# Attention and gated MLP in four chunks: one chunk's input transposed on TensorE instead of by DMA, chunk 0's products in halves, and a new order of the work

## The chip, the core and the metric

The kernel runs on one core of a Trainium2 chip. A core has engines that each work through their own queue of instructions in order: TensorE (PE; its weight loads are shown apart as PEld), VectorE (DVE), ScalarE (ACT), GpSimd (POOL) and SyncE (SP), which here only issues DMAs. They meet through semaphores. The metric is the device time of one execution in microseconds (us): 200.8 is the median of three runs of the kernel before (200.71 to 200.93).

## The reference

One layer on x of 2048 rows by 512 columns, all in bf16:

```python
h  = x + A(layernorm(x))          # attention
h2 = h + B(layernorm(h))          # gated MLP

# A: qkv = x @ wqkv, 32 heads of 16; each row looks at 8 rows: itself and
#    those 2, 4, ... 14 above it (masked where there is none)
logits = einsum("bhsd,bhswd->bhsw", q, k_gathered) * 16 ** -0.5
o = einsum("bhsw,bhswd->bhsd", softmax(logits), v_gathered)
A = o @ wo
# B: F = 1376
gate = x @ W_gate; up = x @ W_up
B = (relu(gate) * up) @ W_down
```

## The kernel before, in words

The 2048 rows are worked in four chunks of 512 (`tk` in the code, "chunk 0" to "chunk 3" here). In a chunk the steps are:

- **Layer norm of x** (`layernorm`, key `x...`): statistics (`bn_stats`, L431, and L434) and the normalised row (L466) on DVE, four tiles of 128 rows. Then the tile is transposed, so that columns stand on partitions. This goes either through TensorE (four 128x128 transposes a tile, L495, and a copy out of the PSUM bank by ScalarE, L511, or for two tiles of chunk 0 by DVE, L509) or by a DMA transpose that SP issues (L484). The table `DMAT` (L348) lists the pairs of tiles that go by DMA; it has chunk 3's x, and the second norm (`h`) of chunks 2 and 3 and half of chunk 1's.
- **Projections** (L536): twelve groups of four matmuls, q and k for four groups of columns in turn and then v, each into a PSUM bank that ScalarE copies out (L544). For the first four groups of chunk 0 (`n < 4`) each group is made in two column halves, rows 0 and 1 of tiles first (`qka`), rows 2 and 3 after (`qkc`), over all four blocks of the weight.
- **Scores**: DVE multiplies q with the four shifted k of one half of the window (L583, `pr`), for two groups of columns at once: 4096 elements a partition. TensorE sums over a head's columns (L589, `sc`, four matmuls of 32 columns at a time), ScalarE takes exp (L619), and for chunk 0 DVE masks (L622, `mk`).
- **Weights back to all columns**: TensorE broadcasts (L689, `bc`) and ScalarE copies (L695) for chunks 0 and 1; for chunks 2 and 3 SP's DMAs do it (L679, `bd`).
- **Weighted v**: DVE multiplies the eight weights with the eight shifted v (L710, `mu`, 4096 elements). The eight are then summed by a tree: its first level (eight to four) is for chunks 0 to 2 a DMA that accumulates, issued by POOL (L742, `ta`), the rest DVE adds (L713, L736), and for chunk 0 a scaling (L717, `om`).
- **Output projection** (L762, `wo`), for chunk 0 with x added by one more matmul (L765), the second layer norm (ScalarE squares, L420), up and gate matmuls (L800) with ScalarE's copies (L804, L807) and DVE's product (L820), the down matmuls (L837), the last addition (L848) and the store (L854).

Every step is recorded first as an `Op` with its engine, planned duration, what it depends on and which buffer of a pool it takes. `Plan.order()` then lays them out: each engine's queue goes by the priorities of the list `RANK`, one number for each recorded step, and the planner picks the next step and a buffer by planned times. The steps are issued in that order, so an instruction waits on its engine for all that stand ahead of it, and the planner's times (`xload`, `wload`, the DMA queue term `dq`) have no effect on the chip but through that order and through the choice of buffers. The one exception is `setup()`, which issues all loads ahead of everything; the weight of q and k comes in four blocks of 128 rows, two issued by SP and two by ScalarE (L294).

So TensorE has in its queue projections of later chunks between the steps of chunk 0's attention, and where they stand decides whether it waits.

Of the kernel before, what the change touches and what calls it, by code (L numbers as in the profile page):

```python
# [8 lines left out]
P = 128  # L9
# [4 lines left out]
ALU = mybir.AluOpType  # L14
# [4 lines left out]
    0, 1, 2, 3, 4, 5, 6, 7, 8, 9, 10, 11, 12, 13, 14, 15, 16, 18, 19, 21,  # L19
    24, 32, 27, 17, 20, 22, 25, 26, 30, 35, 36, 29, 34, 37, 39, 41, 43, 47, 23, 28,  # L20
    31, 33, 38, 45, 48, 42, 59, 65, 40, 51, 55, 46, 56, 60, 49, 52, 57, 73, 76, 61,
    79, 67, 72, 71, 74, 80, 106, 88, 95, 75, 96, 91, 104, 103, 93, 113, 119, 127, 70, 85,
    94, 98, 102, 172, 175, 185, 130, 134, 136, 149, 152, 105, 108, 110, 114, 111, 188, 197, 223, 226,
    231, 179, 190, 217, 221, 228, 171, 180, 208, 211, 219, 158, 169, 195, 207, 210, 245, 252, 236, 241,
    239, 244, 243, 249, 256, 260, 247, 253, 246, 250, 255, 261, 266, 269, 276, 281, 275, 279, 285, 278,
    283, 282, 286, 291, 310, 315, 326, 330, 293, 322, 314, 324, 348, 329, 361, 337, 345, 339, 342, 346,
    350, 365, 333, 358, 349, 354, 340, 352, 353, 356, 363, 323, 328, 316, 321, 302, 313, 308, 312, 332,
    364, 373, 366, 370, 306, 379, 369, 394, 405, 359, 393, 355, 380, 402, 404, 421, 442, 445, 395, 424,
    453, 574, 374, 413, 447, 450, 389, 409, 436, 473, 50, 53, 44, 62, 54, 64, 58, 63, 66, 69,
    77, 90, 78, 83, 92, 81, 87, 82, 86, 89, 118, 129, 157, 170, 124, 196, 164, 178, 97, 101,  # L30
    166, 182, 100, 116, 150, 159, 132, 186, 107, 176, 137, 156, 109, 126, 200, 213, 218, 237, 232, 240,
    251, 258, 262, 264, 274, 284, 287, 288, 296, 294, 292, 298, 300, 307, 305, 309, 303, 318, 327, 360,
    367, 311, 319, 341, 347, 336, 343, 372, 377, 325, 334, 368, 375, 382, 385, 384, 388, 381, 383, 386,
    398, 390, 392, 397, 400, 387, 396, 401, 403, 406, 407, 408, 411, 414, 417, 410, 418, 412, 419, 422,
    457, 467, 434, 484, 477, 480, 461, 481, 491, 472, 475, 429, 466, 449, 460, 441, 476, 478, 433, 435,
    454, 458, 446, 451, 439, 443, 462, 474, 503, 427, 431, 469, 486, 502, 505, 508, 493, 512, 465, 525,
    507, 518, 511, 521, 529, 497, 516, 504, 513, 520, 531, 552, 569, 572, 524, 541, 666, 707, 514, 533,
    537, 540, 536, 539, 580, 708, 112, 120, 99, 121, 68, 84, 115, 122, 125, 133, 144, 163, 147, 160,
    165, 142, 148, 135, 145, 161, 229, 234, 233, 242, 187, 202, 177, 199, 174, 183, 192, 194, 184, 189,
    206, 235, 212, 215, 181, 191, 193, 205, 214, 238, 289, 265, 297, 317, 248, 257, 290, 301, 331, 335,  # L40
    338, 357, 344, 362, 371, 415, 425, 456, 459, 423, 432, 464, 470, 430, 438, 468, 471, 391, 399, 448,
    455, 479, 483, 490, 495, 485, 492, 482, 488, 487, 489, 499, 501, 494, 496, 498, 506, 509, 515, 519,
    522, 526, 528, 527, 534, 517, 532, 596, 601, 562, 594, 565, 589, 558, 591, 604, 544, 553, 542, 551,
    555, 560, 548, 550, 570, 549, 557, 546, 556, 579, 583, 568, 573, 586, 599, 608, 609, 614, 571, 576,
    603, 611, 618, 617, 626, 613, 629, 588, 631, 606, 627, 632, 620, 624, 585, 616, 635, 639, 662, 668,
    672, 623, 641, 643, 677, 628, 636, 638, 675, 634, 637, 645, 647, 117, 141, 128, 139, 131, 140, 123,
    138, 143, 146, 155, 162, 153, 167, 168, 173, 151, 154, 204, 225, 254, 268, 273, 299, 259, 270, 209,
    227, 216, 220, 267, 280, 224, 230, 201, 222, 198, 203, 263, 272, 271, 277, 304, 295, 320, 376, 378,
    351, 416, 420, 426, 428, 437, 444, 440, 463, 452, 530, 535, 543, 561, 500, 510, 523, 566, 547, 554,
    564, 567, 538, 545, 559, 563, 593, 597, 575, 578, 577, 581, 582, 587, 600, 602, 590, 598, 584, 595,  # L50
    592, 605, 607, 610, 619, 622, 615, 625, 621, 633, 612, 630, 657, 689, 683, 687, 667, 673, 671, 680,
    692, 640, 656, 658, 660, 648, 654, 650, 661, 664, 676, 679, 644, 652, 678, 682, 655, 663, 684, 649,
    651, 653, 670, 642, 646, 665, 669, 674, 694, 696, 685, 693, 659, 690, 681, 686, 698, 691, 699, 688,
    697, 701, 710, 714, 717, 719, 705, 709, 711, 715, 695, 702, 704, 706, 700, 703, 712, 713, 716, 718,
    720, 721,
# [36 lines left out]
class Plan:  # L92
# [23 lines left out]
    def order(self):  # L116
# [6 lines left out]
        free = {}  # L123
# [7 lines left out]
        while left:  # L131
# [36 lines left out]
            op.start, op.done = t, t + op.dur + op.lat  # L168
            if op.dq:
                at = max(t + op.dur + op.dq[0], free.get("DQ", 0.0)) + op.dq[1]  # L170
                free["DQ"] = at
                op.done = at + op.lat
            free[op.eng] = t + op.dur
# [18 lines left out]
def kernel(  # L192
# [11 lines left out]
    nc = tc.nc  # L204
# [11 lines left out]
    PRE = ()  # L216
    NAB = 0
# [127 lines left out]
    DAL = 5.5  # L345
    TDD, TDL = 1.25, 1.5
    NWARM, NFILL = 44, 8
    DMAT = (('h',2,0),('h',2,2),('x',3,0),('x',3,2),('h',3,0),('h',3,2),('h',1,0))  # L348
# [11 lines left out]
    HG = ([[0, 1, 2, 3]],) * 4  # L360

# [12 lines left out]
    def load(t):  # L374
        return add(None, "LD", 0.0, None, lat=t)

    xload = [[load(t) for t in (3.5, 3.7, 4.1, 4.35)]] + [[load(t)] * BPC for t in (9.15, 13.2, 15.4)]
    wload = {n: load(t) for n, t in
             (("q", 7.78), ("k", 7.78), ("v", 10.6), ("o", 17.1), ("u", 20.5), ("g", 24.0), ("d", 28.5))}
# [139 lines left out]
    for tk in range(NCK):  # L519
# [10 lines left out]
        for n, (c, t) in enumerate(seq):  # L530
# [3 lines left out]
            def f_mm(lo=0, hi=CS, c=c, t=t, mm=mm, xnT=xnT):  # L534
                for dt in range(NT):
                    nc.tensor.matmul(mm.t[:, lo:hi], lhsT=wv_sb[:, dt, t:D:NT] if c == 2 else wqk_sb[:, dt, c * D + t:(c + 1) * D:NT],  # L536
                                     rhs=xnT.t[:, dt, lo:hi], start=(dt == 0), stop=(dt == NT - 1))
# [9 lines left out]
            if tk == 0 and n < 4:  # L547

                a = None
                for i, (lo, hi, evs) in enumerate(((0, 2 * P, xev[0:2]), (2 * P, CS, xev[2:]))):  # L550
                    a = add(("qk%s%d" % ("ac"[i], n), tk), "PE", 4 * MM * (hi - lo) / CS + 0.02,
                            lambda f=f_mm, lo=lo, hi=hi: f(lo, hi), evs + [wl, a, fills[-1]], pr - 5, take=[mm],
                            use=[xnT], lat=PEL if i == 1 else 0.0)
            else:
                a = add(("qkv%d" % n, tk), "PE", 4 * MM, f_mm, xev + [wl], pr, take=[mm], use=[xnT], lat=PEL)
# [13 lines left out]
        for hf in range(2):  # L569
            sc, ex = Buf(at_s), Buf(ex_s)  # L570
            scd, prd = [], []
            for t in range(0, NT, 2):
# [13 lines left out]
                def f_sc(t=t, sc=sc, pb=pb):  # L586
                    for u in range(2):
# [5 lines left out]
                a = add(("pr%d" % hf, tk), "DVE", D40, f_pr, [d[k] for k in (t, t + 1) for d in (qd, kd, kp)],  # L593
                        apr, take=[pb], use=[qT], lat=DL)
# [312 lines left out]
```

## Time and profile before

| | |
|---|---|
| median of three runs | 200.8 us |
| the profiled execution | 201.23 us, of which the span of its instructions is 199.5 |
| TensorE clock granted | 1.0 of full |
| TensorE from 20 to 180 us, in windows | idle in 1.2 us of 160 |
| VectorE from 20 to 80 us, in windows | idle in 0.6 us of 60 |
| VectorE from 140 to 199.5 us | busy 22.9 us of 59.5 |
| ScalarE | 115.0 us of the span |
| DMA: accumulates issued by POOL | 12 of 512 KB |
| DMA transposes issued by SP | 14, landing 2.5 us after their issue (median) |

A line of the page's group table has the source line, the engine, the operation, what is written and read, the shape and the count; then busy time in all, the mean of one in ns, and how long the engine stood idle just ahead of these instructions and what ended that. Matmuls overlap in the pipeline, so one that lasts 379 ns is followed by the next after 216. The chain of waits goes back from the last instruction to what released it, step by step. A timeline row has the start, the time from first start to last end, engine, line, and the count of instructions merged into it.

### The profile page before, as it was taken

The page shows a single profiled execution, that of the slowest core. Times are in us where ns is not written, and L with a number is a line of the kernel's source. Part 1 is how long each engine was busy: PE and PEld are TensorE (multiplying, and loading weights), DVE is VectorE, ACT ScalarE, POOL GpSimd, SP SyncE. Part 2 cuts the span into 40 slices and gives each one's busy share as a digit, 9 for nine tenths or more (in the row PEclk, how much of TensorE's full clock was granted, in tenths as well). Part 3 has the DMA queues.
Part 4 walks back from the last instruction along what each step waited for, and adds up shares of the span by engine and source line. Part 5 has one row for each costly group of instructions (what it writes and reads, how often), then busy time and mean ns, then how long its engine had stood idle before and what let it go on. Part 6 is the DMA issues. An engine that isn't in the chain of part 4 may idle for free.

```text
span 199.5 us, 2918 instructions
## 1 busy us (share of the span) xinstructions
PE 191.6 (96%) x1080; PEld 95.7 (48%) x1099; DVE 152.6 (77%) x239; ACT 115.0 (58%) x240; POOL 12.6 (6%) x28
## 2 busy tenths in 40 slices
PE   8599999999999999999999999999999999999994
PEld 8385445554445344444444444444444444444542
DVE  6669999999999999998899859999964423032332
ACT  3455899881999987663844557701439620456500
POOL 4000000330000004100113000000000000000000
PEclk9999999999999999999999999999999999999999
DMA  6959981897000008985269970140010130102022
GB/s 166 327 185 324 412 283 32 156 192 148 3 0 0 3 0 157 190 165 123 39 118 196 208 204 2 26 85 20 3 53 0 26 79 0 31 0 79 0 79 79
DMA packets 19981, 20.92 MB, mean 105 GB/s; under 512 B 8608, under 2 KB 16768, under 8 KB 19968
## 3 DMA queue, kind: packets, MB, share of 16 engines
q1 hardware_dynamic: 17520, 13.60, 23.0%
q0 software_dynamic: 1728, 6.29, 16.8%
q10 hardware_dynamic: 720, 0.85, 1.6%
q8 instruction: 8, 0.13, 0.3%
q14 instruction: 5, 0.04, 0.1%
HBM read 8.42 MB, written 2.10 MB: 53 GB/s over the span
## 4 chain that ended last, share of the span: by engine, by line
PE 91%; DMA 4%; ACT 2%; issue 1%; SPq 1%; DVE 0%
PE bank L800 37%; PE bank L536 21%; PE bank L837 19%; PE bank L762 7%; DMA wqk_sb<-in_A_wqkv_dram 4%; PE bank L589 3%; PE bank L495 2%; ACT big L695 1%; PE bank L639 1%; ACT quad L511 1%; PE bank L765 0%; SPq L292 0%; PE bank L689 0%; ACT quad L544 0%; SPq L294 0%
## 5 line engine op out<-in xcount | busy, mean ns | idle before, releaser
L800 PE MATMUL bank<-quad,wu_sb 128*128 128x512 bf16 (+1 forms) x170 | 42.7, 379 | 0.7 <-ACT quad L511 0.3
L800 PE MATMUL bank<-quad,wg_sb 128*128 128x512 bf16 (+1 forms) x173 | 41.6, 379 | 0.1
L837 PE MATMUL bank<-wd_sb,gT 128*128 128x512 bf16 (+3 forms) x184 | 39.4, 366 | 0.2
L807 ACT ACTIVATE gr<-bank 128x512 bf16<-128x512 f32 (+1 forms) x44 | 25.3, 601 | 23.3 <-PE bank L800 21.8
L804 ACT CAST up_sb<-bank 128x512 bf16<-128x512 f32 (+1 forms) x44 | 25.1, 588 | 23.2 <-PE bank L800 22.4
L710 DVE TENSOR_TENSOR big<-big,vT 128x4096 bf16<-128x4096 bf16 x16 | 36.1, 2290 | 0.8 <-DMA big<-ex 0.6
L583 DVE TENSOR_TENSOR big<-quad,kT 128x4096 bf16<-128x4096 bf16 x16 | 36.2, 2288 | 0.4 <-ACT quad L544 0.4
L536 PE MATMUL bank<-quad,wqk_sb 128*128 128x512 bf16 (+1 forms) x140 | 30.3, 356 | 2.1 <-DMA wqk_sb<-in_A_wqkv_dram 1.8
L820 DVE TENSOR_TENSOR gT<-gr,up_sb 128x1024 bf16<-128x1024 bf16 (+1 forms) x24 | 15.2, 646 | 20.5 <-ACT up_sb L804 10.4
L837 PEld LDWEIGHTS <-gT 128*128 128x128 bf16 (+1 forms) x187 | 18.2, 98 | 19.7
L800 PEld LDWEIGHTS <-wu_sb 128*128 128x128 bf16 (+1 forms) x176 | 17.5, 100 | 21.1 <-issue 1.3
L800 PEld LDWEIGHTS <-wg_sb 128*128 128x128 bf16 (+1 forms) x176 | 17.6, 100 | 20.5 <-issue 0.2
L536 PEld LDWEIGHTS <-wqk_sb 128*128 128x128 bf16 x144 | 15.5, 114 | 14.3 <-DMA wqk_sb<-in_A_wqkv_dram 2.3
L848 DVE TENSOR_TENSOR row<-x_sm,bank 128x512 bf16<-128x512 bf16 (+1 forms) x17 | 10.8, 653 | 10.6 <-PE bank L837 10.6
L713 DVE TENSOR_TENSOR big<-big 128x1024 bf16<-128x1024 bf16 (+2 forms) x24 | 17.2, 735 | 0.7 <-DMA big<-big 0.6
L742 POOL DMA_DIRECT2D big<-big x12 | 10.5, 872 | 86.8 <-DVE big L710 42.7
L536 PE MATMUL bank<-quad,wv_sb 128*128 128x512 bf16 x62 | 15.2, 380 | 0.1
L762 PE MATMUL bank<-wo_sb,quad 128*128 128x512 bf16 x63 | 15.2, 379 | 0.1
L466 DVE TENSOR_SCALAR row<-x_sm,mv,rs 128x512 bf16<-128x512 bf16 x32 | 11.6, 407 | 2.3 <-ACT rs L448 2.1
L431 DVE BATCH_NORM_STATS2 st<-x_sm 128x6 f32<-128x512 bf16 x16 | 10.5, 680 | 3.4 <-DMA x_sm<-in_A_x_dram 3.4
L420 ACT ACTIVATE row<-x_sm,mv 128x512 bf16<-128x512 bf16 x12 | 8.6, 723 | 5.0 <-DVE mv L412 5.0
L544 ACT CAST kT<-bank 128x512 bf16<-128x512 f32 x16 | 9.2, 592 | 3.4 <-PE bank L536 3.4
(68 smaller groups left out, 141.6 us busy)
## 6 DMA issues: line engine op xcount, KB each, us to landing
big<-big POOLq DMA_DIRECT2D x12, 512.0 KB, 5.5
big<-ex SPq DMA_DIRECT2D x16, 128.0 KB, 2.8
out_dram<-row SPq DMA_DIRECT2D x15, 128.0 KB, 1.8
x_sm<-in_A_x_dram SPq DMA_DIRECT2D x3, 512.0 KB, 6.4
wu_sb<-in_B_W_up_dram SPq DMA_DIRECT2D x1, 1376.0 KB, 9.7
wg_sb<-in_B_W_gate_dram SPq DMA_DIRECT2D x1, 1376.0 KB, 12.7
wd_sb<-in_B_W_down_dram SPq DMA_DIRECT2D x1, 1280.0 KB, 15.7
wqk_sb<-in_A_wqkv_dram ACTq DMA_DIRECT2D x2, 256.0 KB, 7.2
```

The lines of the kernel that those rows point to most:

```text
L466: V.tensor_scalar(out=xn.t[:], in0=x, scalar1=mv.t[:, j, 0:1], scalar2=rs.t[:, j:j + 1], op0=ALU.add if residual else ALU.subtract, op1=AL ...
L536: nc.tensor.matmul(mm.t[:, lo:hi], lhsT=wv_sb[:, dt, t:D:NT] if c == 2 else wqk_sb[:, dt, c * D + t:(c + 1) * D:NT], rhs=xnT.t[:, dt, lo:h ...
L583: V.tensor_tensor(out=pb.t[:].rearrange("p (t w) s -> p t w s", t=2), in0=q4, in1=k4, op=ALU.mult)
L710: V.tensor_tensor(out=mt.t[:], in0=ab.t[:], in1=v8, op=ALU.mult)
L713: V.tensor_tensor(out=mt.t[:, 0:n, :], in0=mt.t[:, 0:n, :], in1=mt.t[:, n:2 * n, :], op=ALU.add)
L762: nc.tensor.matmul(od.t[:], lhsT=OT.t[:, t, j * P:(j + 1) * P], rhs=wo_sb[:, t, :], start=(t == 0), stop=(t == NT - 1 and tk not in RPE))
L800: nc.tensor.matmul(mm.t[:fs, :], lhsT=w_sb[:, dt, ft * P: ft * P + fs], rhs=hnT.t[:, dt, :], start=(dt == 0), stop=(dt == NT - 1))
L804: nc.scalar.copy(out=ub.t[:fs, i, :], in_=um.t[:fs, :])
L807: nc.scalar.activation(out=gr.t[:fs, i, :], in_=gm.t[:fs, :], func=ACT.Relu)
L820: V.tensor_tensor(out=gt.t[:fs, 0:n, :], in0=gr.t[:fs, 0:n, :], in1=ub.t[:fs, 0:n, :], op=ALU.mult)
L837: nc.tensor.matmul(od.t[:, c0:c1], lhsT=gts[ft].t[:fs, ft % 2, j * P:(j + 1) * P], rhs=wd_sb[:fs, ft, c0:c1], start=(ft == 0), stop=(ft == ...
L848: V.tensor_tensor(out=ob.t[:, c0:c1], in0=x_sm[:, tk * BPC + j, c0:c1], in1=od.t[:, c0:c1], op=ALU.add)
```

## The change

Three things change in the recorded steps, and with them the order of everything:

1. Chunk 3's x leaves `DMAT`: its four tiles are transposed by sixteen TensorE transposes, with two ScalarE copies, and four DMA transposes on SP go.
2. Chunk 0's first four projection groups are made in three parts: both column halves over weight blocks 0 and 1 only (`qka`, `qkc`, two matmuls of 256 columns each, which wait for those two blocks alone), then the full width over blocks 2 and 3 (`qkd`).
3. Chunk 0's q*k products (`PRS`) and weight*v products (`MUH`) are made by two instructions of 2048 elements each in place of one of 4096. A q*k half needs one group of q and k; a weight*v half needs one half of the window.

The planner's load times and its model of the DMA queue are changed too, and `RANK` is a new list (737 numbers in place of 722). The further options `PRD`, `DAC2` and `HSP` come in with empty lists.

```diff
-    DMAT = (('h',2,0),('h',2,2),('x',3,0),('x',3,2),('h',3,0),('h',3,2),('h',1,0))
+    DMAT = (('h',2,0),('h',2,2),('h',3,0),('h',3,2),('h',1,0))
+    PRS, MUH = (0,), (0,)
...
-            def f_mm(lo=0, hi=CS, c=c, t=t, mm=mm, xnT=xnT):
-                for dt in range(NT):
+            def f_mm(lo=0, hi=CS, d0=0, d1=NT, c=c, t=t, mm=mm, xnT=xnT):
+                for dt in range(d0, d1):
                     nc.tensor.matmul(mm.t[:, lo:hi], lhsT=...,
-                                     rhs=xnT.t[:, dt, lo:hi], start=(dt == 0), stop=(dt == NT - 1))
+                                     rhs=xnT.t[:, dt, lo:hi], start=(dt == 0 and lo == 0), stop=(dt == NT - 1))
...
-                a = None
+                ab, done = [wload["ab"]], []
                 for i, (lo, hi, evs) in enumerate(((0, 2 * P, xev[0:2]), (2 * P, CS, xev[2:]))):
-                    a = add(("qk%s%d" % ("ac"[i], n), tk), "PE", 4 * MM * (hi - lo) / CS + 0.02,
-                            lambda f=f_mm, lo=lo, hi=hi: f(lo, hi), evs + [wl, a, fills[-1]], pr - 5, take=[mm],
-                            use=[xnT], lat=PEL if i == 1 else 0.0)
+                    done.append(add(("qk%s%d" % ("ac"[i], n), tk), "PE", 2 * MM * (hi - lo) / CS + 0.005,
+                                    lambda f=f_mm, lo=lo, hi=hi: f(lo, hi, 0, 2), evs + ab + done + [fills[-1]], pr - 5,
+                                    take=[mm], use=[xnT]))
+                a = add(("qkd%d" % n, tk), "PE", 2 * MM, lambda f=f_mm: f(0, CS, 2, NT), done + [wl], pr - 4.9, take=[mm],
+                        use=[xnT], lat=PEL)
...
+                if tk in PRS:
+                    def f_p1(u, t=t, hf=hf, pb=pb, qT=qT, s0=s0):
+                        kb = kT[:, t + u, PADL + s0 - 4 * hf * DIL: PADL + s0 - 4 * hf * DIL + CS]
+                        k4 = bass.AP(tensor=kb.tensor, offset=kb.offset,
+                                     ap=[list(kb.ap[0]), [-DIL, 4]] + [list(y) for y in kb.ap[1:]])
+                        V.tensor_tensor(out=pb.t[:, 4 * u:4 * u + 4, :],
+                                        in0=qT.t[:, t + u, :].unsqueeze(1).to_broadcast([P, 4, CS]), in1=k4, op=ALU.mult)
+                    for u in range(2):
+                        a = add(("pr%d%s" % (hf, "ac"[u]), tk), "DVE", D20, lambda u=u, f=f_p1: f(u),
+                                [d[t + u] for d in (qd, kd, kp)], apr, take=[pb], use=[qT], lat=DL)
...
+            if tk in MUH:
+                def f_m1(hf, t=t, ab=ab, mt=mt, s0=s0):
+                    vb = vT[:, t, PADL + s0 - 4 * hf * DIL: PADL + s0 - 4 * hf * DIL + CS]
+                    ...
+                    V.tensor_tensor(out=mt.t[:, 4 * hf:4 * hf + 4, :], in0=ab.t[:, 4 * hf:4 * hf + 4, :], in1=v4, op=ALU.mult)
+                ms = [add(("mu%d%s" % (t, "ac"[hf]), tk), "DVE", D20, lambda hf=hf, f=f_m1: f(hf),
+                          [x for x in abd if x.key[0][2] == str(hf)] + vds, tpr, take=[mt], use=[ab], lat=DL) for hf in range(2)]
```

What the order does with it, by engine. On TensorE, all four tiles of chunk 0 are transposed ahead of the first q/k group (before, two were behind the first two groups); chunk 3's transposes stand among chunk 2's projections; chunk 0's output projection comes after four of chunk 3's twelve projection groups in place of six; chunk 2's first scores and chunk 1's first broadcast, which followed each other, have the transposes of two tiles between them; and between chunk 0's second transposes and its first up matmul there now stand two broadcasts, one projection and one score group, where there were a broadcast and a score group. On VectorE, the copy L509 of tile 3 comes ahead of chunk 1's statistics, chunk 0's half products follow each other in another order, and chunk 2's statistics go behind chunk 0's first products. On SP, chunk 3's broadcasts go out ahead of all of chunk 0's stores. POOL's twelve accumulates stay, in another order within chunks 1 and 2.

## The prediction, made before the changed kernel had run

> **What bounds the kernel now.** I read the page's busy table first, then the chain that ended last, then windows and the timeline at the places where the chain leaves the matmuls, and last the DMA landings.
>
> ```profile
> span 199.5 us, 2918 instructions
> PE 191.6 (96%) x1080; PEld 95.7 (48%) x1099; DVE 152.6 (77%) x239; ACT 115.0 (58%) x240; POOL 12.6 (6%) x28
> PE 91%; DMA 4%; ACT 2%; issue 1%; SPq 1%; DVE 0%
> ```
>
> The chain is TensorE (PE) nearly from end to end. What PE doesn't do is wait for the first weights, in the chain in order of time (start, length, what) and in PE's timeline:
>
> ```profile
> 2.16 7.84 DMA wqk_sb<-in_A_wqkv_dram
> 10.05 0.85 PE bank L536 x6
> 10.89 0.45 PE bank L495 x8
> 64.90 0.47 ACT quad L511
> ```
>
> ```profile
> 8.66 0.41 PE L536 MATMUL bank<-quad,wqk_sb 128*128 128x256 bf16 x2 [0.85 <-DMA wqk_sb<-in_A_wqkv_dram]
> 10.05 0.85 PE L536 MATMUL bank<-quad,wqk_sb 128*128 128x256 bf16 x6 [0.98 <-DMA wqk_sb<-in_A_wqkv_dram]
> 53.23 1.03 PE L762 MATMUL bank<-wo_sb,quad 128*128 128x512 bf16 x4
> 66.88 1.02 PE L800 MATMUL bank<-quad,wu_sb 128*128 128x512 bf16 x3 [0.27 <-ACT quad L511]
> ```
>
> Two of four weight blocks are there at 8.66, and PE uses them for two matmuls only; the other two come at 10.05. Behind that PE is full, so the end is set by (a) how much PE work is left at 10.05, and (b) whether VectorE (DVE) feeds it in time. DVE has little room up to the first output projection (L762, 53.23), as the window from chunk 1's x to the end of chunk 0's attention shows:
>
> ```profile
> core 0: us, PE busy (x) PEld busy (x) DVE busy (x) ACT busy (x) POOL busy (x), PEclk, DMA share, GB/s
> 11.15:52.18 41.03, 40.76 (x261) 21.98 (x264) 40.13 (x62) 31.08 (x61) 3.76 (x5) 1.00 0.75 207
> ```
>
> ```profile
> 35.41 6.69 DVE L710 TENSOR_TENSOR big<-big,vT 128x4096 bf16<-128x4096 bf16 x3
> 51.43 0.75 DVE L717 TENSOR_TENSOR quad<-big,rec 128x512 bf16<-128x512 bf16 x2
> ```
>
> ```profile
> L710 DVE TENSOR_TENSOR big<-big,vT 128x4096 bf16<-128x4096 bf16 x16 | 36.1, 2290 | 0.8 <-DMA big<-ex 0.6 <-issue 0.2
> L713 DVE TENSOR_TENSOR big<-big 128x2048 bf16<-128x2048 bf16 x4 | 4.9, 1222 | 0.1
> ```
>
> The profiled execution took 201.23 us, its span 199.5; the median of the runs shown is 200.8. I sum differences against the profiled execution and carry them to the median.
>
> **PE work, part by part.** *Start.* In the new order the transposes of rows 2 and 3 stand before the first q/k matmul, and each of the four q/k banks first gets its products over weight blocks 0 and 1. PE then has, before 10.05, eight transposes (0.45, chain row) and ten 256-column matmuls (eight first halves, one bank's second pair; 0.109 each by start times at 10.3 to 10.6): 0.45 + 1.09 = 1.54 in place of today's two (0.22): 1.32 us of work is gone from behind 10.05. It fits: the two rows leave DVE at 7.97 and 8.35 (L466), so their transposes end at about 8.6; their two copies (0.59 and 0.41, on ScalarE and DVE) end by about 9.4, before the second pair wants them; 8.66 + 1.09 = 9.75. Sixteen of 32 half-width matmuls become eight full ones: 16 x 0.109 - 8 x 0.216 = 0.02 less.
>
> *Stalls of today that lose their cause.* By matmul start times PE loses 0.17 at 12.2 (VectorE's copy L509 stands behind a bn_stats that waits for x; now ahead of it) and 0.22 at 14.2 (a bank): 0.39. At 66.9 and 69.3 it loses 0.33 and 0.18 to the copy L511 of chunk 0's transposes: there the new order puts a score group, two broadcasts and a projection between the last transposes and the first up matmul (about 2.7 us against 1.5), more than the two copies need (2 x 1.02): 0.51.
>
> *Chunk 3's transposes.* 16 more on PE. The chain has eight in 0.45, so 0.056 each: +0.89. They need two more ScalarE copies (1.016 each); ScalarE is busy 7.38 of 12.18 between 40 and 52.18, so they hide; if that cover went they would cost at most 2.0. Four DMA transposes leave SP's queue (1.2 each); SP is otherwise idle there, so nothing directly. *Order.* Chunk 2's scores and chunk 1's broadcast no longer touch, so one more change between the packed form and full matmuls: 0.10 by start times (0.31 against 0.216). Gate, up, down and output counts are unchanged.
>
> PE alone: -1.32 - 0.02 - 0.39 - 0.51 + 0.89 + 0.10 = -1.25.
>
> On transposes there is a rule against the change: the Trainium skill, "TensorE: Matmul & The Clock Gate", Part 4, gives about 275 ns for one in a kernel. By it, sixteen would be an estimated 4.4 us. The chain's 0.056 decides here, since they run in a row.
>
> **VectorE, which takes some of it back.** Chunk 0's eight 4096-element products become sixteen of 2048. Three big ones in a row take 6.69, so they start 2.20 apart, 0.09 under their duration; a 2048 one, 1.222 long, then starts every 1.135. A split costs 2 x 1.135 - 2.20 = 0.07, eight of them 0.54. Bounds: nothing below (a gain by starting earlier is counted next), and 2 x 1.222 - 2.290 = 0.154 each, 1.23, if the tails don't overlap; I take 0.54, since they follow one another without waits. The Trainium skill, "VectorE: DVE Perf Modes", section "The DRAIN you can't avoid", says the next op waits until the pipe is empty; by it the sum takes the larger bound. The 2.20 spacing speaks against that.
>
> DVE ends chunk 0's last scaling (L717) at 52.18. The copy L509 (0.32) moves ahead of the stretch. Idle is 41.03 - 40.13 = 0.90, and four waits each hide a 0.09 tail, 1.26; the halves let the products start on one bank's q and k, and chunk 2's statistics go behind them, so I take 1.05 of it as gone. New end: 52.18 - 0.32 - 1.05 + 0.54 = 51.35.
>
> PE's first output projection is moved ahead of two of chunk 3's projections (2 x 0.863) and behind its transposes: 53.23 - 1.32 - 0.02 - 0.39 - 1.73 + 0.89 = 50.66 if nothing held it. Its input comes at 51.40. So PE waits 0.74, and everything behind it on PE with it. Chunk 3's transposes stand shortly ahead and wait for rows that DVE makes late too; that is the same lateness, not a second one. Between no wait and the 1.6 that the upper price of the halves and 0.2 less recovered idle give, I take 0.74.
>
> **Sum:** -1.25 + 0.74 = -0.51: 200.7 for the profiled execution, 200.3 for the median. 0.2% of 200.8 is 0.4 us, about what a measurement can tell from no change.
>
> **Queues that things move past.** POOL's twelve accumulating DMAs stay, but the first two of chunk 0 are issued about 1.1 apart, after half products, not 2.5. Their landings:
>
> ```profile
> DMA to landing us min/median/max: 4.5/5.5/7.0
> ```
>
> On SP, chunk 3's weight broadcasts go out before three of chunk 0's output stores and before chunk 2's last accumulate; in that stage now their issue stretches to 1.36 (0.61 median) beside accumulates. Today that accumulate landed after 6.57 with broadcasts behind it, 1.1 over the median, and chunk 2's first output projection began 3.5 after the landing; with that room I cost it at 0, up to 1.1. Of the output rows only the last ones set the end, and those keep their form.
>
> **Rivals.** *A, slower: the accumulate lands late.* After chunk 0's first accumulate is issued, DVE has four half products (4.54), four small aggregates, one bn_stats (0.60) and a normalisation (0.32) before the sum that needs it: 5.8, less 0.6 from product to issue, 5.2. Today it landed after 5.20, with DMA transposes in flight beside it; those are gone, and the first of chunks 1 and 2 took 4.5 and 4.7. If it took the stage's longest, 7.04, DVE would stop for 1.8 and pass that to PE's output projection: -0.51 + 1.84 = +1.3, 202.1. It decides from 0.9 us of lateness (slower), from 0.1 (no longer faster). For it: the two come closer together, and successive ones land 2.5 to 3.3 apart. Against it: the missing transposes.
>
> *B, same: DVE swallows the early start.* Chunk 1's x lands at 11.13 whatever PE does, so DVE's chain starts there. With the halves at 1.23, or the idle kept, the wait at the output projection is 1.2 to 1.6: -0.05 to +0.35, 200.7 to 201.2.
>
> *C, faster still: no wait at L762.* If halves cost nothing and all idle goes, 0 to 0.3 of wait is left: -1.25 to -0.95, 199.6 to 199.9.
>
> *D, slower: transposes cost their duration.* 0.219 each by the group row of L495: 16 x 0.163 = 2.6 more, 202.9. The eight in 0.45 speak against it; that is also where the skill's 275 ns would lead.
>
> *E, slower: broadcasts and accumulates of chunks 2 and 3 collide*, the 1.1 above with no room left for it: 201.4.
>
> **Chances.** Forecast case 0.43 (200.0 to 200.4), C 0.09, B 0.22, A 0.19, D 0.02, E 0.05. Faster by over 0.2%: forecast and C, 0.52. Within: B, 0.22. Slower: 0.26. The range reaches from C's end, 199.6, into A up to 201.6, 1.3 us of lateness; what A has beyond that, and D, are left out. The forecast's own range is 200.0 to 200.5.
>
> **What would show it.** PE's first q/k matmul still at about 8.7, ten half-width ones before 10.05 and no gap after; 88 transposes instead of 72 with eight still in 0.45; ten DMA transposes; the half products starting about 1.13 apart; the first output projection at about 51.4, preceded by a wait for DVE. An accumulate landing more than 5.2 after its issue, with DVE idle before the tree sum, means A; first output projection later than 52.2 means B. The forecast is wrong if PE waits anywhere behind 70.

## The result

The changed kernel takes 202.61 us (median of 5 executions, 202.51 to 203.33) where the kernel before took 200.8: ratio 1.010, 95% interval 1.008 to 1.012. Run again beside other versions it was 202.82 against 200.57, ratio 1.012 (1.010 to 1.014). It is slower by 1.8 to 2.3 us. The forecast was 200.3, with 201.6 as the upper end and "slower" at 0.26: wrong in sign and outside the range.

The profiled execution took 203.33 us. Its page, with the lines that answer to those shown of the kernel before:

```profile
span 201.6 us, 2978 instructions
PE 194.5 (97%) x1107; PEld 95.7 (47%) x1107; DVE 152.6 (76%) x247; ACT 117.2 (58%) x242; POOL 12.7 (6%) x28
PE 43%; DVE 35%; DMA 9%; issue 8%; ACT 3%; POOL 0%; DVEq 0%; POOLq 0%; ACTq 0%
L914 PE MATMUL bank<-wd_sb,gT 128*128 128x512 bf16 (+3 forms) x187 | 40.8, 367 | 1.4 <-DVE gT L897 1.4
L762 DVE TENSOR_TENSOR big<-big,vT 128x4096 bf16<-128x4096 bf16 x12 | 27.2, 2284 | 2.5 <-DMA out_dram<-row 2.5
big<-ex SPq DMA_DIRECT2D x16, 128.0 KB, 4.1
```

The row of the kernel before that answers to the last of these:

```profile
big<-ex SPq DMA_DIRECT2D x16, 128.0 KB, 2.8
```

The shares of busy time hardly tell the two kernels apart, but the chain does: TensorE carried 91% of it before and 43% now, VectorE 35% in place of 0, so what ended last now hangs on work that reaches TensorE late. Two idle times are new. VectorE stood 2.5 us ahead of a weighted v (L762, before L710), and TensorE 1.4 ahead of a down matmul (L914, before L837). And the weight broadcasts, issued by SP (`big<-ex`), now land 4.1 us after their issue in the middle, where it was 2.8.

TensorE's timeline shows the start and the places where it stops:

```profile
7.85 0.78 PE L516 MATMUL bank<-identity,row 128*128 128x128 bf16 x8 [0.22 <-DVE row L487]
8.46 4.71 PE L557 MATMUL bank<-quad,wqk_sb 128*128 128x256 bf16 x28
...
56.49 1.05 PE L612 MATMUL bank<-big,sel 128*32 128x512 bf16 x16 [0.37 <-DVE mv L433]
59.79 0.38 PE L690 MATMUL bank<-ex,same 128*128 128x512 bf16 x1 [0.19 <-ACT ex L670]
...
127.84 2.33 PE L914 MATMUL bank<-wd_sb,gT 128*128 128x512 bf16 x10 [1.36 <-DVE gT L897]
```

The start does what was forecast: q/k matmuls from 8.46 on and no pause at the second pair of weight blocks. By matmul start times TensorE then loses 0.45 at 15.2, 0.44 at 56.5, 0.35 at 59.8, 0.24 around 63.7, 1.52 at 127.8 and 0.25 at 142.4. The one at 127.8 is the largest. VectorE's timeline, and the chain from 109 on, lead back from it:

```profile
115.31 0.69 DVE L765 TENSOR_TENSOR big<-big 128x1024 bf16<-128x1024 bf16 x1 [0.62 <-DMA big<-big]
118.95 2.29 DVE L762 TENSOR_TENSOR big<-big,vT 128x4096 bf16<-128x4096 bf16 x1 [2.49 <-DMA out_dram<-row]
```

```profile
109.15 6.14 DMA big<-big
115.28 0.02 issue
115.31 0.70 DVE big L765
...
116.36 2.56 DMA out_dram<-row
118.92 0.03 issue
118.95 2.29 DVE big L762
```

An accumulate is in flight from 109.15 to 115.28; the tree sum that needs it waits 0.62. Then chunk 3's first weighted v (`3.mu3`, 118.95) waits 2.49. The profile names a store as what ended that wait, but the product doesn't read what a store writes; it reads the broadcast weights, all eight of them, and the last two landed at 118.43 and 118.77. The view of the broadcasts' issues in that stretch (duration of an issue in ns, then the time to landing) and SP's timeline:

```profile
L730 SPq DMA_DIRECT2D big<-ex x8: 550/1184/2083, 105.3 to 114.9; - x8
DMA to landing us min/median/max: 3.9/5.7/7.0
```

```profile
105.28 10.21 SPq L730 DMA_DIRECT2D big<-ex  x8
115.59 1.95 SPq L931 DMA_DIRECT2D out_dram<-row  x2
```

Accumulates are issued at 105.04 and 109.15, and SP issues the eight broadcasts from 105.28 on, between and behind them. In the kernel before, SP first had two stores and began the broadcasts at 110.34; they landed after 3.1 us (median), and VectorE wanted them only at 122.7, behind chunk 2's second norm:

```profile
L679 SPq DMA_DIRECT2D big<-ex x8: 612/618/1361, 110.3 to 116.9; - x8
DMA to landing us min/median/max: 2.6/3.1/4.9
122.74 2.29 DVE L710 TENSOR_TENSOR big<-big,vT 128x4096 bf16<-128x4096 bf16 x1 [0.22 <-issue]
```

The last of them landed there at 120.57, later than the 118.77 of the changed kernel, and nothing waited for it. So a late landing is half of the matter; the other half is how early it is wanted. In the changed kernel `3.mu3` stands ahead of chunk 2's second norm on VectorE, ScalarE's squares for that norm (from 122.61) stand ahead of chunk 1's last up copies (from 126.49), and the product of those (L897, 127.09) is what TensorE waits for at 127.84.

So there were two theories. Theory 1: the new order puts broadcasts beside accumulates, they land late, and VectorE's queue hands the lateness on. Theory 2: the three parts themselves cost it, and the late waits are only where it shows.

### The profile page after: what moved, and what is told of

Read it like the earlier page. It is cut to its first block, busy times and chain, and to the rows that moved or that the text cites. A ratio compares the mean times of both kernels' runs of the same rounds, so it can differ in the third digit from the quotient of the medians.

```text
span 201.6 us, 2978 instructions
## 1 busy us (share of the span) xinstructions
PE 194.5 (97%) x1107; PEld 95.7 (47%) x1107; DVE 152.6 (76%) x247; ACT 117.2 (58%) x242; POOL 12.7 (6%) x28
## 4 chain that ended last, share of the span: by engine, by line
PE 43%; DVE 35%; DMA 9%; issue 8%; ACT 3%; POOL 0%; DVEq 0%; POOLq 0%; ACTq 0%
PE bank L869 25%; PE bank L914 10%; DVE big L762 6%; DVE big L765 5%; DMA x_sm<-in_A_x_dram 5%; DVE big L621 4%; DVE st L452 4%; DVE big L777 3%; DVE big L606 3%; DVE row L487 3%; DMA big<-big 3%; PE bank L831 3%; DVE x_sm L842 2%; PE bank L557 2%; PE bank L612 1%
## 5 line engine op out<-in xcount | busy, mean ns | idle before, releaser
L869 PE MATMUL bank<-quad,wg_sb 128*128 128x512 bf16 (+1 forms) x176 | 42.4, 379 | 0.0
L914 PE MATMUL bank<-wd_sb,gT 128*128 128x512 bf16 (+3 forms) x187 | 40.8, 367 | 1.4 <-DVE gT L897 1.4
L897 DVE TENSOR_TENSOR gT<-gr,up_sb 128x1024 bf16<-128x1024 bf16 (+1 forms) x24 | 15.2, 643 | 27.4 <-ACT gr L876 14.8
L762 DVE TENSOR_TENSOR big<-big,vT 128x4096 bf16<-128x4096 bf16 x12 | 27.2, 2284 | 2.5 <-DMA out_dram<-row 2.5
L914 PEld LDWEIGHTS <-gT 128*128 128x128 bf16 (+1 forms) x187 | 18.0, 98 | 21.9 <-DVE gT L897 2.2
L606 DVE TENSOR_TENSOR big<-quad,kT 128x4096 bf16<-128x4096 bf16 x12 | 27.2, 2283 | 0.0
L557 PEld LDWEIGHTS <-wqk_sb 128*128 128x128 bf16 x136 | 14.7, 114 | 12.0 <-issue 1.3
L532 ACT COPY quad<-bank 128x1024 bf16<-128x1024 bf16 (+1 forms) x11 | 10.4, 954 | 3.8 <-PE bank L516 3.8
```

The costliest lines, as they stand in the source:

```text
L606: V.tensor_tensor(out=pb.t[:].rearrange("p (t w) s -> p t w s", t=2), in0=q4, in1=k4, op=ALU.mult)
L762: V.tensor_tensor(out=mt.t[:], in0=ab.t[:], in1=v8, op=ALU.mult)
L869: nc.tensor.matmul(mm.t[:fs, lo:hi], lhsT=w_sb[:, dt, ft * P: ft * P + fs], rhs=hnT.t[:, dt, lo:hi], start=(dt == 0), stop=(dt == NT - 1))
L897: V.tensor_tensor(out=gt.t[:fs, 0:n, :], in0=gr.t[:fs, 0:n, :], in1=ub.t[:fs, 0:n, :], op=ALU.mult)
L914: nc.tensor.matmul(od.t[:, c0:c1], lhsT=gts[ft].t[:fs, ft % 2, j * P:(j + 1) * P], rhs=wd_sb[:fs, ft, c0:c1], start=(ft == 0), stop=(ft == ...
```

## The experiments

Each time is a median, and each ratio is to the kernel before in executions beside it, with a 95% interval.

| kernel | parts | order | us | ratio |
|---|---|---|---|---|
| before | none | old | 200.5 to 200.8 | 1 |
| changed | 1, 2, 3 | new | 202.61; 202.82 | 1.0100 (1.0081 to 1.0118); 1.0120 (1.0099 to 1.0141) |
| noacc | 1, 2, 3, two accumulates out | new | 201.16 | 1.0038 (1.0017 to 1.0059) |
| h95 | 1, 2, 3 | new to 95 us | 201.73 | 1.0066 (1.0041 to 1.0091) |
| h1 | 1, 2, 3 | new to 68 us | 201.13 | 1.0032 (1.0015 to 1.0050) |
| h1hn | 1, 2, 3 | as h1, one step moved | 201.25 | 1.0022 (1.0001 to 1.0043) |
| h1m2 | 1, 3 | as h1 | 202.00 | 1.0071 (1.0054 to 1.0088) |
| h1f | 2, 3 | as h1, VectorE's changed | 207.62 | 1.0344 (1.0295 to 1.0394) |
| p1 | 1 | old | 202.19 | 1.0087 (1.0058 to 1.0117) |
| p3 | 3 | old | 200.99 | 1.0010 (0.9986 to 1.0034) |
| p23 | 2, 3 | old behind 18 us | 199.36 | 0.9938 (0.9923 to 0.9954) |
| p123 | 1, 2, 3 | old behind 18 us | 200.57 | 1.0002 (0.9986 to 1.0018) |

**Two accumulates taken away.**

```diff
-                    def f_da(mt=mt):
-                        nc.gpsimd.dma_start(mt.t[:, 0:4, :], mt.t[:, 4:8, :], accum_op=ALU.add)
+                    def f_da(mt=mt, out=(tk, t) in ((2, 0), (2, 1))):
+                        if not out:
+                            nc.gpsimd.dma_start(mt.t[:, 0:4, :], mt.t[:, 4:8, :], accum_op=ALU.add)
```

> The changed kernel with the two last-issued accumulating DMAs of chunk 2 (column groups 1 and 0) left out, so that these two groups of chunk 2 sum only the first half of their window; everything else, the order included, is that of the changed kernel. Theory 1 (chunk 3's eight broadcasts go out just behind these two accumulates, share the DMA engines with them, and land late): the broadcasts land about 2.6 to 3.2 us after their issue in place of 5.7 to 7.0, VectorE's wait of 2.49 ahead of chunk 3's weighted v at 119 and the 0.62 at 115.3 shrink to under 0.3 in all, and with them TensorE's wait of 1.52 ahead of the down matmuls at 128; the time falls by 1.2 to 2.3 us, to 200.3 to 201.4. Theory 2 (the loss is in the early parts, the transposes and the halves, and the late waits are only where it shows): broadcasts may land earlier, but the time stays at 202.3 or more.

Measured: 201.16, ratio 1.0038 against 1.0100 and 1.0120. The same two views of this kernel, and its group of weighted v:

```profile
L730 SPq DMA_DIRECT2D big<-ex x8: 542/558/604, 105.5 to 110.0; - x8
DMA to landing us min/median/max: 2.6/2.6/2.8
```

```profile
105.48 5.09 SPq L730 DMA_DIRECT2D big<-ex  x8
```

```profile
L762 DVE TENSOR_TENSOR big<-big,vT 128x4096 bf16<-128x4096 bf16 x12 | 27.2, 2284 | 0.0
big<-ex SPq DMA_DIRECT2D x16, 128.0 KB, 2.6
```

Issued at the same time and in the same order, the broadcasts now land 2.6 us after their issue in place of 5.7, SP is through with them in 5.09 in place of 10.21, VectorE doesn't wait at L762, and TensorE has no wait at all behind 65. The last broadcast lands at 112.79 in place of 118.77, 6.0 us earlier: it is issued 4.9 earlier (109.96, not 114.89) and lands 1.1 sooner after its issue (2.83, not 3.89). So the larger part of the lateness is that SP's issuing is held up. The ratio falls by 0.006 to 0.008: 1.2 to 1.6 us (each plus or minus 0.6) of the 2.0 to 2.4 that the changed kernel lost by its ratios. Theory 1 holds for that part. The 0.62 of the tree sum at 115.31, which waited for one of the two accumulates itself, is gone with them, and noacc doesn't tell it from the broadcasts' 2.49. What is left, 0.6 over the kernel before, theory 1 doesn't explain.

**The old order behind some point.** These two have all of the change and differ from the changed kernel in `RANK` alone. Of the changed order they keep what is planned up to 95 us (h95) or 68 us (h1); behind that the steps come in the order of the kernel before:

```diff
 SP, around chunk 3's broadcasts
-3.bd (8 broadcasts), 0.os (stores)
+0.os, 0.os, 3.bd (8 broadcasts), 0.os
 VectorE
-2.tree0, 3.mu3, 2.rs .. 2.hnm, 3.mu2, 2.hxn, 1.gu0
+2.tree2, 1.gu1, 2.rs .. 1.gu0 .. 2.hnm, 3.mu1, 1.gu3, 2.hxn
```

> The changed kernel with all three parts of the change and its order up to about 95 us; behind that, the order of the kernel before. Chunk 3's broadcasts are thereby issued behind chunk 2's accumulates and behind two of chunk 0's stores, and VectorE has chunk 3's weighted v later, behind the second norm of chunk 2. Theory 1 (collision of broadcasts and accumulates, whose lateness VectorE passes on because chunk 3's weighted v stands ahead of what chunks 1 and 2 need): no VectorE wait over 0.5 us at chunk 3's weighted v and no TensorE wait over 0.4 us behind 100; 200.0 to 201.3. Theory 2 (early parts cost it): 202.2 to 202.8, with TensorE idle somewhere behind 100 as before.

> The changed kernel with all three parts of the change and its order up to about 68 us, behind that the order of the kernel before, chunks 1, 2 and 3 thus fed as before. Theory 1 (late collision): TensorE waits as in the changed kernel up to 68 (about 1.3 us in all) and as in the kernel before behind it (under 0.3): 199.8 to 200.8. Theory 2 (the early parts make the loss): 202.2 to 202.8. If h1 is faster than the version with the order kept to 95 us, something between 68 and 95 costs too.

Measured: h95 201.73, h1 201.13. In both the broadcasts are issued behind the accumulates and VectorE's idle time ahead of L762 is 0.2 in place of 2.5; in h1 TensorE waits nowhere behind 64. The broadcasts of h1 and its first weighted v of chunk 3:

```profile
L730 SPq DMA_DIRECT2D big<-ex x8: 602/627/1564, 109.7 to 116.6; - x8
DMA to landing us min/median/max: 2.7/3.4/4.3
122.27 2.29 DVE L762 TENSOR_TENSOR big<-big,vT 128x4096 bf16<-128x4096 bf16 x1 [0.22 <-issue]
```

The last one lands at 119.34, again later than in the changed kernel, and is not wanted before 122.27. So theory 1 gains again, by about 1.5 in h1. With noacc, where the weights are wanted as early as in the changed kernel but land in time, this says that the loss needs both, weights wanted early and landing late; no run moves `3.mu3` alone. But neither theory's numbers fit: h1 was to be at most 200.8. And h95 misses by 0.4 on the upper side. Its TensorE timeline names a stop that h1 doesn't have:

```profile
104.04 1.89 PE L869 MATMUL bank<-quad,wg_sb 128*128 128x512 bf16 x8 [0.38 <-DMA quad<-row]
```

It is the same mechanism in another place. In h95 an accumulate of chunk 2 is issued at 97.80 and the DMA transposes of chunk 1's second norm at 98.84 and 101.01; they land 4.47 and 2.90 us after their issue (2.5 alone), and TensorE loses 0.54 (by start times) waiting for them. In h1 the accumulate goes out at 96.28, the transposes land after 2.85 and 2.50, and nothing waits.

**The parts one by one.** p1 and p3 are the kernel before with one part; in h1m2 part 2 is taken out of h1.

```diff
 p1 (kernel before)
-    DMAT = (('h',2,0),('h',2,2),('x',3,0),('x',3,2),('h',3,0),('h',3,2),('h',1,0))
+    DMAT = (('h',2,0),('h',2,2),('h',3,0),('h',3,2),('h',1,0))
 p3 (kernel before)
+    PRS, MUH = (0,), (0,)
 h1m2 (h1)
-                    done.append(add(("qk%s%d" % ("ac"[i], n), tk), "PE", ..., lambda ...: f(lo, hi, 0, 2), ...))
-                a = add(("qkd%d" % n, tk), "PE", 2 * MM, lambda f=f_mm: f(0, CS, 2, NT), done + [wl], ...)
+                    a = add(("qk%s%d" % ("ac"[i], n), tk), "PE", ..., lambda ...: f(lo, hi), evs + [wl, a, fills[-1]], ...)
```

> The kernel before with part 1 alone: chunk 3's x transposed by TensorE and copied by ScalarE, four DMA transposes fewer, the order otherwise the old one with the transposes put in shortly behind the rows they need. Both theories have TensorE full there, so sixteen transposes at 0.056 cost 0.89 and a wait for the rows some tenths: 201.6 to 202.2, 0.9 to 1.3 over the kernel before. If transposes cost their full duration (0.219 each), 2.6 more: 204. If the fewer DMA transposes give something back by earlier landings of the accumulates, 200.8 to 201.2.

> The kernel before with part 3 alone: chunk 0's eight products of 4096 elements each made by two of 2048 right behind each other, the order as it was. VectorE's own work grows by eight times 0.07 (forecast) to 0.154 (upper bound): its last scaling of chunk 0 comes 0.5 to 1.2 later than in the kernel before, and the 2048-element products start 1.13 apart. TensorE has some 0.6 of room there, so the time rises by 0 to 0.6: 200.5 to 201.1.

> The version with the changed kernel's order to 68 us and the old one behind (201.13 in its own runs, call it the hybrid), with part 2 taken out: chunk 0's first four groups again over all four weight blocks in column halves, in the same places of the order, so that TensorE can't begin before the last block lands (9.1 to 10.0 in the executions so far, 8.5 in the hybrid). Theory 3 (the early start is worth what lies between 8.5 and the landing, less than the 1.32 of the forecast, since the profile of before had the latest landing of all): 0.4 to 1.2 over the hybrid, 201.5 to 202.3, and a wider spread between executions than the hybrid's 0.33. Theory 4 (VectorE swallows the early start on its way to the first output projection): 201.1 to 201.3, with TensorE's waits around 56 to 64 gone or shorter in their place.

Measured: p1 202.19, which is 1.65 over before (by the interval 1.2 to 2.3), at the upper edge of what was expected. The span of its instructions is only 1.0 longer (median 199.7 against 198.7): in p1 and h1m2 alone, some executions have 2.0 to 3.0 us outside the span, where those of all other kernels have 1.7 to 1.9, and the record doesn't show what that is. In p1's profile TensorE also waits 0.41 at 19.4 for a row of chunk 1; its weights had landed 0.5 earlier than in the profile of before, so this needn't be part 1's. p3 200.99: no difference that can be told (ratio up to 1.0034), as expected; its half products start 1.135 apart, as forecast, but chunk 0's last scaling ended at 51.95, 0.2 earlier than in the profile of before and not 0.5 to 1.2 later (chunk 1's x had landed 0.3 earlier in that execution). h1m2 202.00: without the early start h1 is 0.8 slower (0.0039 in ratio; 0.5 by the spans, each against the kernel before beside it), and TensorE's waits at 56 to 64 are still there, so VectorE doesn't swallow it (theory 4 falls). Its TensorE timeline has the wait back:

```profile
8.53 0.38 PE L557 MATMUL bank<-quad,wqk_sb 128*128 128x256 bf16 x2
9.40 3.80 PE L557 MATMUL bank<-quad,wqk_sb 128*128 128x256 bf16 x27 [0.48 <-DMA wqk_sb<-in_A_wqkv_dram]
```

And its executions spread over 1.5 us (201.25 to 202.75; the spans over 1.4), where those of h1 spread over 0.33.

**What h1 still loses.** In the changed kernel and in h1 alike, VectorE stands idle behind chunk 0's attention while a product that is ready waits behind a small step. The lines are of the changed kernel's VectorE timeline:

```profile
50.55 2.28 DVE L606 TENSOR_TENSOR big<-quad,kT 128x4096 bf16<-128x4096 bf16 x1
54.08 0.15 DVE L433 TENSOR_SCALAR mv<-sm 128x1 f32<-128x1 f32 x1 [1.24 <-ACT x_sm L840]
54.15 2.28 DVE L606 TENSOR_TENSOR big<-quad,kT 128x4096 bf16<-128x4096 bf16 x1
```

The product at 54.15 is the one that TensorE waits for at 56.49.

```diff
 VectorE, h1
-1.pr1, 0.hnm, 1.pr1, 0.hnm, 0.hnm, 2.pr0
+1.pr1, 1.pr1, 0.hnm, 0.hnm, 0.hnm, 2.pr0
 ScalarE, h1
-0.rs3, 1.ex0, 0.rs1, 0.hsq, 0.rs2, 3.qe0, 0.hsq, 0.rs0, 3.qe7, 0.hsq, 1.ex1, 0.hsq
+0.rs3, 1.ex0, 0.rs1, 0.rs2, 3.qe0, 0.rs0, 0.hsq, 0.hsq, 1.ex1, 3.qe7, 0.hsq, 0.hsq
```

> The hybrid with one thing moved: chunk 0's small steps of the second norm, which on VectorE stand ahead of chunk 1's last q*k product and wait there for ScalarE's statistics of the output projection (VectorE idle 1.24 at 52.4 in the hybrid), go behind that product, and ScalarE's squares and exps are put in the matching order. All parts of the change stay. If that wait on VectorE is what TensorE's waits at 56.1, 59.4 and 63.2 to 63.5 come from (0.41, 0.35 and 0.24, 1.0 in all, in the changed kernel too), they go: 200.1 to 200.5. If they have another cause, 200.9 to 201.3, with the waits elsewhere by then.

Measured: 201.25; by ratio no difference from h1 (1.0022 against 1.0032). TensorE's waits at 56, 59 and 63 went from 1.0 to 0.09, and came back 4 us later. Of the two lines of h1hn the first is TensorE's timeline and the second the window 60 to 70 (PE, PEld, DVE, ACT, POOL busy):

```profile
67.09 0.93 PE L741 MATMUL bank<-ex,spread 32*128 32x512 bf16 x4
```

```profile
60.00:70.00 10.00, 9.71 (x81) 4.34 (x80) 9.83 (x11) 10.00 (x23) 0.00 (x0) 1.00 0.01 2
```

A group of broadcast matmuls that took 0.39 in h1 and in the changed kernel takes 0.93, since its banks must first be copied out, and ScalarE is busy for all of the window. h1hn begins this group 0.56 ahead of h1 (67.09, 67.65) and the up matmuls behind it 0.14 after h1 (68.14, 68.00). So the waits at 56 to 64 were real but not the bound; in h1hn's trace it is ScalarE's copies that the banks wait for around 67.

**Part 1 taken out of h1.** Chunk 3's x goes by DMA transposes again, issued behind chunk 3's normalised rows, which stand among chunk 0's weighted v:

```diff
-    DMAT = (('h',2,0),('h',2,2),('h',3,0),('h',3,2),('h',1,0))
+    DMAT = (('h',2,0),('h',2,2),('x',3,0),('x',3,2),('h',3,0),('h',3,2),('h',1,0))
 VectorE
-0.mu3a, 0.mu3c, 0.mu2a, .. 3.xxn, .. 0.mu0a, 3.xxn, 3.xxn, 3.xxn
+0.mu3a, 0.mu3c, 3.xxn, 3.xxn, 3.xxn, 3.xxn, 0.mu2a, ..
```

> The hybrid with part 1 taken out: chunk 3's x goes by DMA transposes again; VectorE normalises chunk 3's rows before the second pair of chunk 0's weighted v so that the transposes leave early, and one of chunk 3's projections moves ahead of chunk 0's output projection. If TensorE is the bound there, the sixteen transposes' 0.89 come off the hybrid: 200.2 to 200.5. If VectorE is (theory 4), TensorE waits up to 0.9 for chunk 0's scaled sums and nothing is gained: 200.9 to 201.3; with DMA transposes and accumulates in each other's way it could be slower than that.

Measured: 207.62. The view of the four transposes, and TensorE's timeline:

```profile
L505 SPq DMA_TRANSPOSE quad<-row x4: 1309/2390/3357, 34.2 to 40.6; - x4
DMA to landing us min/median/max: 4.7/7.0/9.4
```

```profile
50.15 1.87 PE L557 MATMUL bank<-quad,wv_sb 128*128 128x512 bf16 x4 [4.92 <-DMA quad<-row]
```

All four are in flight beside chunk 0's accumulates (issued at 34.19, 36.63, 39.13 and 41.40) and land 4.7 to 9.4 us after their issue, and TensorE waits 4.9 for the last. It doesn't end there. The page's row of the granted clock, in tenths of full and 40 slices of 5.1 us, dips at that place:

```profile
PEclk9999999997599999999999999999999999999999
```

From 48.96 to 55.79 the granted clock is 0.5 of full, and up to there TensorE's matmuls start every 0.43 us in place of 0.216, 2.7 us more behind a wait of 5.1 (both by start times); the six executions have a mean clock of 0.983 to 0.984, and no other run's trace has such a stretch between its first projection and its last matmul. The two less the 1.3 that part 1 costs (below) are 6.5; h1f is 6.3 slower than h1 by ratio. The expected 200.2 to 201.3 left the collision out but for half a sentence, and the clock altogether. In the kernel before three of the four are issued ahead of the first accumulate (35.76) and took 2.5; the fourth, behind it, took 5.3.

**The parts in the old order.** p23 is the kernel before with parts 2 and 3, in the new order up to 18 us and the old one behind; its DMA transposes are issued at 31.05 to 35.06, the first accumulate at 34.51. p123 adds part 1.

```diff
 p23 (kernel before; with qkd and the halves as in the change)
+    PRS, MUH = (0,), (0,)
 p123 (p23)
-    DMAT = (('h',2,0),('h',2,2),('x',3,0),('x',3,2),('h',3,0),('h',3,2),('h',1,0))
+    DMAT = (('h',2,0),('h',2,2),('h',3,0),('h',3,2),('h',1,0))
```

> The kernel before with parts 2 and 3 and without part 1: the new order up to about 18 us of the plan, behind that the old one, chunk 3's x by DMA transposes at their old places (issued from 32 on, mostly ahead of the first accumulate). If part 1 is what makes the early parts a loss (alone it cost 1.65, while the early start was worth 0.87 in the hybrid), the early start now comes out as a gain: 199.8 to 200.4, 0.3 to 0.9 under the kernel before. If VectorE or ScalarE swallow it, or the accumulates, which now come earlier, run into the DMA transposes: 200.5 to 201.5, with TensorE waiting for chunk 3's transposed rows or for chunk 0's scaled sums.

> The changed kernel once more, beside the kernel before on the same chip as the version without part 1, so that the differences stand side by side: 202.3 to 203.0; broadcasts of chunk 3 landing 5 to 7 us after their issue again, and TensorE's wait of about 1.5 at 128 again.

> All three parts of the change in the old order: the version with parts 2 and 3 (199.36, ratio 0.9938) with part 1 added, chunk 3's x transposed on TensorE shortly behind its rows, and nothing else moved. If part 1's price is its sixteen transposes on a full TensorE (0.89) and one more change of form (0.10), with the two copies hidden: 200.2 to 200.6, the same as the kernel before. If it is what it cost alone (1.65): 200.8 to 201.3, about the hybrid's time, and then of the changed kernel's 2.0 over before some 0.4 is parts and 1.6 is order. If the parts together lose the whole 2.0: 202.3 or more.

Measured: p23 199.36, ratio 0.9938 (0.9923 to 0.9954), the fastest of all, 1.7% under the changed kernel and 0.4 better than the best that was expected; p123 200.57, ratio 1.0002; the changed kernel again 202.82, with the broadcasts landing 3.3 to 7.2 us after their issue. Its wait at 127 was 0.87 there, less than the 1.5 expected. The page of p23:

```profile
span 197.8 us, 2909 instructions
PE 191.1 (97%) x1071; PEld 94.7 (48%) x1091; DVE 152.6 (77%) x247; ACT 114.6 (58%) x240; POOL 12.7 (6%) x28
PE 92%; DVE 2%; ACT 2%; DMA 1%; issue 1%
big<-ex SPq DMA_DIRECT2D x16, 128.0 KB, 2.6
```

The chain is TensorE again, now without the 4% that were the wait for weights. So the three parts together, in the old order, change nothing that can be told (p123); part 1 costs 1.3 (0.0064 in ratio) and parts 2 and 3 give 1.2. All of the changed kernel's loss, 2.0 to 2.4, is the new order: about 0.6 up to 68 us (h1 against p123; by the intervals 0.1 to 1.1) and 1.4 to 1.8 behind.

## Why the prediction was wrong

**The step that failed** is the one that prices the broadcasts on SP: "Today that accumulate landed after 6.57 with broadcasts behind it, 1.1 over the median, and chunk 2's first output projection began 3.5 after the landing; with that room I cost it at 0, up to 1.1." It asks how late the accumulate gets, and who waits for that. The late ones were the broadcasts: 5.7 us (median) in place of 2.6, by noacc, the last of them issued 4.9 later as well; the step had the row of the stretched issue (1.36 against 0.61) and didn't price it. And who waits was read from the old order, where VectorE wants the broadcasts at 122.7; the changed order wants them at 116.4, and has chunk 2's norm and chunk 1's last products queued behind. It cost 1.2 to 1.6. Rival E had this collision, still with the accumulate as the late one: its 1.1 is near the 1.2 to 1.6, its 201.4 too low by the rest below, and its chance of 0.05 too small. "The forecast is wrong if PE waits anywhere behind 70" is what happened, at 127.84.

**The start and its stalls** (-1.32 - 0.02 - 0.39) were right in what they describe, as the timeline from 8.46 on shows; against p3, which has no early start, p23 gains 1.4 (0.0072 in ratio). A tenth of it was misread: of the 0.22 at 14.2, 0.11 is a matmul whose record the trace lacks (its weight load at 14.00 is there). And in the changed kernel 0.45 comes back at 15.2, where TensorE, being earlier, waits for a row of chunk 1. What failed is to carry the sum to the median. In the profiled execution of before (201.23) the last weight block landed at 10.00; in the twelve later profiles (all kernels have the same loads) it landed between 8.13 and 9.95. That the old start pays for this from one execution to the next and the new one doesn't is argued from the spreads: 24 executions of before spread from 199.28 to 201.19, those of p123 over 0.36, and h1m2 against h1 says the same; the landing is on record for the profiled executions only. By that the sum was made against a late execution, 0.4 to 0.7 over the median (200.5 to 200.8), and that much of the gain isn't there. The forecast's own terms without those of the order (-1.32 - 0.02 - 0.39 + 0.89 + 0.10 = -0.74) give 200.49 for p123's profiled execution; it took 200.59.

**Sixteen transposes** at 0.89, with 0.10 for one more change of form: 1.3, plus or minus 0.4, by p123 against p23. Right within that; rival D's 2.6 more is excluded. The Trainium skill, "TensorE: Matmul & The Clock Gate", Part 4, gives about 275 ns for a transpose, by which sixteen would be an estimated 4.4 us. That is the duration of one; those here follow each other 0.056 us apart, and the runs decide against 4.4.

**The halves** at 0.07 each: the 1.135 between starts was measured as forecast, and p3 shows no cost beyond 0.0034 in ratio, 0.7 us. The rule of the Trainium skill, "VectorE: DVE Perf Modes", section "The DRAIN you can't avoid", that the next operation waits until the pipe is empty, would have them an estimated 1.22 apart. The trace disagrees; the prediction left out that the same section lets an operation that isn't held start earlier.

**The wait of 0.74 at the first output projection** didn't occur: VectorE was through with chunk 0's scaling at 50.63, not 51.35, so "I take 1.05 of it as gone" was too careful (0.2 of the difference is luck: chunk 1's x landed at 10.92, not 11.13). Rivals A and B fall with it; the accumulates of chunk 0 landed in time. In its place VectorE waited 1.24 for ScalarE's statistics of that projection and TensorE lost 1.0 between 56 and 64, which the forecast had not looked for.

**The stalls at 66.9 and 69.3** (-0.51) are gone in the changed kernel, as forecast, but the time isn't gained: in h1hn TensorE's banks wait around 67 for ScalarE's copies. The two additional copies were costed at nothing because ScalarE had room "between 40 and 52.18". In the window 60 to 70 of before it was busy for 9.92 of 10. That this is what h1 loses against p123 (0.6) is argued from that window and from h1hn, not shown: no run took ScalarE's work out of it.

Of the miss of 2.3 (202.6 against 200.3), then, 1.2 to 1.6 is the collision and 0.4 the late execution that the sum was made against (201.23 against 200.8). The remaining 0.3 to 0.7 fits with the new order up to 68 us, which costs 0.6 where the forecast's -0.51 and +0.74 made 0.23, and with part 1's 1.3 in place of 0.99; the cause of the 0.6 stays open.

## What to carry to other kernels

Read a moved DMA by what is in flight when it will be issued, and by the first instruction that reads what it brings in the *new* order, with everything queued behind that one; a landing time from the old order says nothing of either. Before a sum is made against a profiled execution, see how late its loads landed: where the change hides a load, take the gain against a usual landing, not against this one. And cover for added copies has to be looked for in every window up to the next point where TensorE needs the copier, not only in the one where the copies stand.

## What the runs showed of the hardware

DMAs that SP issued while an accumulate from POOL was in flight landed later, and their issue itself was held up. Eight broadcasts of 128 KB landed after 2.6 us without and 5.7 with it (medians, noacc against the changed kernel), and SP needed 5.09 and 10.21 for issuing them. DMA transposes landed after 2.5 without and up to 9.4 beside four accumulates (h1f). An accumulate isn't the only cause of a late landing: chunk 2's eight broadcasts, in the changed kernel and with no accumulate issued while they flew, landed after 2.5 to 4.3. The accumulates suffered less: 6.1 and 6.4 beside the broadcasts, against 4.5 to 5.8 for chunk 1's, which have none; the third of chunk 2, 6.36 there, took 5.29 in h1, where the broadcasts begin as it lands. The Trainium skill, "DMA: Bandwidth & Descriptors", section "SWDGE vs HWDGE vs iDMA", says that the two kinds of queue are served in turn inside each DMA engine; that both get slower agrees with it, but no run here shows the turns, nor why the smaller transfers lose more.

Behind a wait of 5.1 us, TensorE worked at half the granted clock: 0.5 of full from 48.96 to 55.79 in h1f, matmuls of 512 columns every 0.43 us in place of 0.216. Waits up to 1.5 us (the changed kernel, at 127.8) left the clock at 1.0.
